# A list scheduler's priorities: one turn a task in place of due times shared by groups

## The chip, the cores and the metric

One core of one Trainium2 chip. The metric is the device time of one execution in microseconds (us). A kernel's time is the median of its runs; the profile is of one execution.

## The reference

Two layers in a row. First, attention with a narrow window: 8 batches, 8 heads, 576 positions, 64 channels. Heads 0 to 3 see the last 32 positions, heads 4 to 7 every fourth of the last 128. Second, a gated feed-forward layer on the 8 heads put side by side.

```python
scores = scale * np.matmul(q, k.transpose(0, 1, 3, 2))
scores = np.where(masks[None, :, :, :], scores, -1000000000.0)
attn = np.exp(scores - np.max(scores, axis=-1, keepdims=True))
attn = attn / (np.sum(attn, axis=-1, keepdims=True) + 1e-09)
x = np.matmul(attn, v)            # then heads side by side: (8, 576, 512)
h = np.maximum(x @ w_in, 0.0)     # 512 -> 1024
conv_out = conv_w[0] * h[s-1] + conv_w[1] * h[s] + conv_w[2] * h[s+1]   # along the positions
gate = 1.0 / (1.0 + np.exp(-conv_out))
out = (h * gate) @ w_out          # 1024 -> 512
```

## The kernel before

The kernel is written as a list of 2032 tasks, each one instruction or a small run of them, with an engine, a cost in us, the tasks it comes after, the buffers it uses and a due time. A planner in the kernel's own Python puts them in one order, and the instructions are emitted in it; every engine then works through its own part in that order.

**Attention** (`attention`, L225 on). A head group is two heads of one batch, four groups a batch, numbered here 0 to 31. Its tasks: loads of `qk` (L231) and `v` (L233) on SP's queue; S, the scores, 72 small matmuls (L243); mask (L254) and max (L256) on VectorE; then for groups 0 to 7 the exponentials by slots on ScalarE, 9 activations with 9 reads of the accumulator (L263), for the others a subtraction, one exponential (L271) and a sum; reciprocal (L276), product (L277) and transpose (L279) on VectorE; V, the values, 80 or 84 small matmuls (L295). V's result leaves PSUM as a rounded half `x..a` (ScalarE, L318) and the rest `x..b`: for groups 0 to 7 by a correction on TensorE (L322) and a ScalarE copy (L325), else by a VectorE subtraction (L330). S and V share one PSUM slot (`att`): the next S or V waits until the one before has been read out, S by the mask, V by `x..a` and `x..b`.

**Feed-forward** (`expert`). The first layer of a batch has 16 groups (8 blocks `fc` of 128 outputs, two halves of the positions), each of 4 pieces of 3 matmuls of 288 columns (L355), a piece for each head group. A group holds one of two PSUM slots `mm` (some of batch 0 take `nn`) until ScalarE's relu to `h` (L362). The gate of a block: the middle tap on ScalarE (L373), two taps on VectorE (L367), sigmoid on ScalarE (L378), product on VectorE (L380), rounded half on ScalarE (L382) and the rest `lo` on VectorE (L384). The second layer has 4 or 5 groups a batch, each of 8 pieces of 3 matmuls of 512 columns (L400), a piece for each block; a group holds one of two slots `nn` until ScalarE's copy `out` (L410), which is then stored from SP's queue. In batch 0 the groups are cut in halves of 256 columns.

**Weights** come as 64-bit numbers and are rebuilt: for each of 8 blocks (`weights`) one load of 1 MB, one Abs (L464) and one copy (L472) on ScalarE, and seven instructions on VectorE (L465 to L479). The conv weights (`few_weights`) are a small load, one Abs and six short VectorE instructions (L435 to L445).

**The planner** (`Planner`). `start` says when a task could start: after the last one on its engine and what it depends on, and when a buffer slot of its pool comes free. `order` takes, engine by engine, the ready tasks whose start is within `WINDOW` (0.25 us) of the earliest, and of these the one with the lowest due time; of the engines the one whose earliest start comes first. Due times come from the table `DUE`, one number for each group of tasks (a batch's first layer, a batch's gates, a head group's softmax and so on), with fixed steps inside a group:

```python
first = min(x[0] for x in at)
s, t = min((x for x in at if x[0] <= first + self.WINDOW), key=lambda x: (x[1].due, x[0]))
```

Tasks are made in this order: weights of the first layer, conv weights, weights of the second layer, the 32 head groups, the 8 batches of the feed-forward part.

Of the kernel before, what the change touches and what calls it, by code (L numbers as in the profile page):

```python
# [56 lines left out]
QK = 2 * S + 32  # L57
# [3 lines left out]
DUE = {  # L61
    "first": (74.70, 81.70, 357.10, 189.80, 929.80, 83.60, 71.70, 1180.10),
    "gated": (93.60, 342.20, 358.10, 9.30, 1117.90, -60.20, -25.30, 36.00),
    "second": (24.50, 424.40, 452.80, 855.50, 1126.50, 1620.90, 1602.90, 1506.70),
    "weights": (82.70, 1550.20, 2380.40, 91.90, 97.30, -18.10, 171.90, 69.10),
    "fetch": (69.90, 42.80, -64.40, -60.40, 72.60, 97.70, 1233.60, 1550.60),
    "conv": 351.60,
    "scores": ((20.00, 1789.40, 129.10, 41.40), (1611.70, 17.90, -51.70, 73.80), (403.50, 353.80, 96.90, 65.70), (270.80, 69.10, 12.90, 80.10), (837.10, -73.40, 77.90, 140.80), (49.80, 977.60, -11.00, 940.00), (1183.10, 95.90, -34.70, 1535.50), (-103.80, 98.20, 411.50, 1557.60)),
    "softmax": ((6.00, -38.50, 7.80, 431.60), (-12.40, 25.50, 0.40, -12.70), (462.70, 1197.90, 365.00, 75.40), (1485.50, 93.40, -17.30, 1003.90), (41.70, 95.80, 1003.50, 910.00), (-44.30, 1543.80, 79.70, 1832.30), (155.80, 89.90, 461.20, 95.80), (94.80, 301.00, -37.60, 31.70)),
    "values": ((842.50, -107.30, -8.70, 6.60), (-23.40, 4.00, 78.20, 43.70), (-4.50, -87.40, -34.50, 89.10), (3.90, 19.10, 32.20, 128.20), (29.70, 66.00, 347.10, -61.20), (-8.50, 1.60, 347.80, 17.20), (961.30, 71.70, 1044.10, 41.10), (22.90, 1623.60, 1475.90, 138.10)),  # L70
    "queries": ((-194.00, -340.50, -87.70, -64.20), (-95.90, 10.40, 59.30, -61.10), (22.90, 138.40, 114.70, 206.60), (959.30, 835.80, 807.00, 1024.00), (1038.20, 1322.20, 1022.30, 1286.00), (1424.90, 492.20, 1554.20, 1412.20), (1489.70, 1710.00, 973.30, 1772.10), (1810.40, 2547.40, 2385.70, 1573.80)),
    "runs": ((-49.30, -20.50, -64.40, -5.70), (40.70, 36.00, 37.60, -38.70), (33.20, 97.00, 48.60, 47.50), (945.80, 351.90, 61.40, 98.30), (456.80, 1101.70, 167.50, 1221.90), (1380.70, 843.50, 1173.90, 1550.10), (1874.10, 1571.80, 1233.90, 1624.20), (1797.40, 2410.30, 1564.00, 1555.00)),
}
# [9 lines left out]
class Task:  # L83
    def __init__(self, engine, cost, due, run, after, uses, table):
        self.engine, self.cost, self.due, self.run, self.table = engine, cost, due, run, table
        self.after, self.uses, self.end = [t for t in after if t is not None], list(uses), None
        for b in self.uses:
            b.left += 1


class Planner:
# [38 lines left out]
    def order(self):  # L130
# [9 lines left out]
        while len(done) < len(self.tasks):  # L140
            best = None
            for e, ts in ready.items():
# [5 lines left out]
                s, t = min((x for x in at if x[0] <= first + self.WINDOW), key=lambda x: (x[1].due, x[0]))  # L148
# [26 lines left out]
def attn_moe(ctx: ExitStack, tc: tile.TileContext, qk_p, qk_d, v_p, v_d, w_in, w_out, conv, mask, out):  # L175
# [49 lines left out]
    def attention(b, p):  # L225
        due, soft, val = SCORES[b][p], SOFTMAX[b][p], VALUES[b][p]
# [4 lines left out]
        lq = plan.add("SP", QK * 0.0017, QUERIES[b][p], lambda: nc.sync.dma_start(  # L231
            out=qk.t, in_=(qk_p, qk_d)[kind][b, p % 2]), uses=[qk])
        lv = plan.add("SP", 1.35, RUNS[b][p], lambda: nc.sync.dma_start(  # L233
# [14 lines left out]
        last = plan.add("PE", 0.75, due, scores, [lq], [qk, sc, s], "S")  # L248
# [5 lines left out]
        last = plan.add("DVE", 0.75, soft + 0.0, lambda: nc.vector.tensor_tensor(  # L254
            out=flat(), in0=scored(), in1=masked, op=ALU.add), [last], [sc, s])
        last = plan.add("DVE", 0.755, soft + 0.5, lambda: nc.vector.tensor_reduce(  # L256
            out=m.t, in_=flat(), axis=AX.X, op=ALU.max, negate=slotwise), [last], [s, m])
        if slotwise:
            last = plan.add("ACT", 0.23, soft + 1.0, lambda: nc.scalar.mul(out=m.t, in_=m.t, mul=SCALE), [last], [m])
# [6 lines left out]
            last = plan.add("ACT", 3.1, soft + 1.5, exps, [last], [s, m, z], "exp")  # L266
            last = plan.add("ACT", 0.23, soft + 2.1, lambda: nc.scalar.add(out=z.t, in_=z.t, add=1e-9), [last], [z])
        else:
            last = plan.add("DVE", 0.755, soft + 1.0, lambda: nc.vector.tensor_tensor(
                out=flat(), in0=flat(), in1=wide(m.t), op=ALU.subtract), [last], [s, m])  # L270
            last = plan.add("ACT", 0.685, soft + 1.5, lambda: nc.scalar.activation(  # L271
                out=flat(), in_=flat(), func=AF.Exp, scale=SCALE), [last], [s], "exp")

            last = plan.add("DVE", 0.765, soft + 2.0, lambda: nc.vector.tensor_reduce(
# [57 lines left out]
        return [plan.add("DVE", 0.77, val + 1.5, low, [last], [tv, x])]  # L332


    TERMS = ((0, 0), (0, 1), (1, 0))
# [241 lines left out]
```

## Time and profile before

| | |
|---|---|
| median of 3 runs | 520.24 us |
| the three runs | 517.2, 520.24, 523.06 us |
| the profiled execution's own time (its span, first to last instruction) | 517.2 us |
| TensorE matmuls busy | 489.6 us, 7464 matmuls |
| VectorE busy | 389.6 us, 552 instructions |
| ScalarE busy | 302.9 us, 623 instructions |
| bytes moved by DMA | 50.96 MB, 99 GB/s on average |

PE is TensorE, PEld its weight loads, DVE is VectorE, ACT ScalarE, SP the engine whose queue holds the loads and stores (SPq). Matmuls are pipelined and their ends are modelled, so a short wait of TensorE may not show as idle time; the distance from one matmul's start to the next one's does show it.

### The profile page before, as it was taken

To read this page: it belongs to the slowest core of one execution; us is meant where nothing else is said; L and a number is where in the kernel's file an instruction comes from. 1 tells how busy PE (TensorE), PEld (TensorE's weight loads), DVE (VectorE), ACT (ScalarE), POOL (GpSimd) and SP (SyncE) were. 2 spreads that over 40 slices of the span, in tenths; PEclk is the share of its full clock that TensorE was granted. 3 is DMA by queue.
4 is the path that set the end of the run, shared out by engine and by line. 5 is a ranking of instruction groups with operands and counts; after the bars stand their busy time and mean duration, and the time that the engine had idled before them with its cause. 6 is when DMAs were issued, how large, how long until landed. Compare 5 with 4: busy or idle time off the path is not lost.

```text
span 517.2 us, 16516 instructions
## 1 busy us (share of the span) xinstructions
PE 489.6 (95%) x7464; PEld 435.8 (84%) x7464; DVE 389.6 (75%) x552; ACT 302.9 (59%) x623; POOL 1.4 (0%) x27
## 2 busy tenths in 40 slices
PE   3379999999999999999999999999999999999996
PEld 2278999999778998799878997899977899889985
DVE  4998999999986999739970599738999479318800
ACT  5967989738432777158741686438632388327710
POOL 1000000000000000000000000000000000000000
PEclk9999999999999999999999999999999999999999
DMA  8866442212255420412132213421244200110011
GB/s 302 292 210 249 166 158 99 69 41 69 90 161 162 135 80 20 151 53 91 53 105 72 68 50 109 142 82 50 95 126 126 74 1 1 42 42 1 1 61 41
DMA packets 16549, 50.96 MB, mean 99 GB/s; under 512 B 2016, under 2 KB 3168, under 8 KB 15456
## 3 DMA queue, kind: packets, MB, share of 16 engines
q1 hardware_dynamic: 16336, 49.84, 28.9%
q8 instruction: 58, 0.95, 0.8%
q10 hardware_dynamic: 144, 0.08, 0.1%
q14 instruction: 11, 0.09, 0.1%
HBM read 40.48 MB, written 9.44 MB: 97 GB/s over the span
## 4 chain that ended last, share of the span: by engine, by line
PE 88%; ACT 8%; DMA 2%; DVE 1%; issue 1%; ACTq 0%
PE nn L400 38%; PE mm L355 36%; PE att L295 6%; PE att L243 5%; ACT s L263 3%; PE nn L355 3%; ACT c L378 1%; ACT L378 1%; DMA qk<-in_qk_p_dram 1%; PE att L322 1%; DMA v<-in_v_d_dram 1%; ACT h L362 0%; DVE c L380 0%; ACT t L464 0%; DVE c L367 0%
## 5 line engine op out<-in xcount | busy, mean ns | idle before, releaser
L400 PE MATMUL nn<-wo,g 128*128 128x512 f32 (+1 forms) x960 | 210.9, 375 | 0.0
L400 PEld LDWEIGHTS nn<-wo,g 128*128 128x128 f32 x960 | 164.6, 188 | 32.1 <-ACT out L410 0.4
L367 DVE SCALAR_TENSOR_TENSOR c<-h,conv_sb,c 128x576 f32<-128x576 f32 x128 | 103.2, 814 | 42.5 <-ACT c L373 41.5
L362 ACT ACTIVATE h<-mm 128x288 f32<-128x288 f32 x120 | 48.1, 406 | 36.4 <-PE mm L355 36.3
L410 ACT COPY out<-nn 128x512 f32<-128x512 f32 (+1 forms) x40 | 21.7, 542 | 63.0 <-PE nn L400 59.2
L355 PE MATMUL mm<-x6a,wi 128*128 128x288 f32 x192 | 54.5, 298 | 0.2 <-ACT h L362 0.2
L380 DVE TENSOR_TENSOR c<-c,h 128x576 f32<-128x576 f32 x64 | 47.7, 756 | 6.8 <-ACT c L378 6.0
L382 ACT CAST g<-c 128x576 fp32r<-128x576 f32 x64 | 42.6, 672 | 17.3 <-DVE c L380 17.2
L373 ACT ACTIVATE c<-h,conv_sb 128x576 f32<-128x576 f32 x64 | 49.6, 777 | 3.7 <-DVE g L384 2.2
L378 ACT ACTIVATE c<-c 128x576 f32<-128x576 f32 x64 | 43.1, 683 | 12.4 <-DVE c L367 11.6
L384 DVE TENSOR_TENSOR g<-c,g 128x576 fp32r<-128x576 f32 x64 | 47.8, 756 | 2.4 <-ACT g L382 1.4
L295 PEld LDWEIGHTS att<-pt,v 32*64 32x64 f32 x2624 | 32.2, 135 | 18.0 <-issue 7.9
L243 PE MATMUL att<-qk 64*32 64x64 f32 x2304 | 33.3, 238 | 12.4 <-DMA qk<-in_qk_p_dram 7.4
L243 PEld LDWEIGHTS att<-qk 64*32 64x32 f32 x2304 | 27.4, 112 | 19.7 <-DVE s L254 5.4
L295 PE MATMUL att<-pt,v 32*64 32x64 f32 (+1 forms) x2624 | 35.9, 235 | 7.8 <-DVE z L276 5.2
L355 PE MATMUL mm<-x2a,wi 128*128 128x288 f32 x144 | 40.9, 299 | 1.0 <-issue 1.0
L355 PE MATMUL mm<-x3a,wi 128*128 128x288 f32 x144 | 40.8, 299 | 0.2 <-ACT h L362 0.2
L355 PE MATMUL mm<-x1a,wi 128*128 128x288 f32 x144 | 40.3, 296 | 0.0
L355 PEld LDWEIGHTS mm<-x6a,wi 128*128 128x128 f32 x192 | 36.1, 188 | 0.9 <-ACT h L362 0.4
L355 PE MATMUL mm<-x5a,wi 128*128 128x288 f32 x128 | 36.4, 299 | 0.2 <-ACT h L362 0.2
L355 PE MATMUL mm<-x0a,wi 128*128 128x288 f32 x112 | 32.4, 306 | 0.0
L355 PE MATMUL mm<-x6b,wi 128*128 128x288 f32 x96 | 28.4, 296 | 0.0
(119 smaller groups left out, 775.9 us busy)
## 6 DMA issues: line engine op xcount, KB each, us to landing
qk<-in_qk_p_dram SPq DMA_DIRECT2D x16, 592.0 KB, 4.0
qk<-in_qk_d_dram SPq DMA_DIRECT2D x16, 592.0 KB, 4.1
out_dram<-out SPq DMA_DIRECT2D x28, 256.0 KB, 2.0
v<-in_v_d_dram SPq DMA_DIRECT2D x16, 384.0 KB, 3.3
v<-in_v_p_dram SPq DMA_DIRECT2D x16, 384.0 KB, 3.4
raw<-in_w_in_dram SPq DMA_DIRECT2D x4, 1024.0 KB, 6.9
raw<-in_w_out_dram SPq DMA_DIRECT2D x4, 1024.0 KB, 6.0
out_dram<-out SPq DMA_DIRECT2D x16, 128.0 KB, 2.3
```

Of the source, the lines that this page charges most:

```text
L243: nc.tensor.matmul(sc.t[quad * 32:quad * 32 + 32, o:o + W], qk.t[hd * 64:hd * 64 + 64, q0:q0 + 32], qk.t[hd * 64:hd * 64 + 64, S + q0:S + ...
L295: nc.tensor.matmul(tv.t[hd * 64:hd * 64 + 64, o:o + hi - lo], v.t[quad * 32:quad * 32 + 32, i, hd * 64:hd * 64 + 64], pt.t[quad * 32:quad ...
L355: nc.tensor.matmul(ps.t[:, 0:HALF], wi[jw][fc // 2][:, fc % 2, k], x[k].t[jx][:, hf * HALF:hf * HALF + HALF], start=(k == 0 and i == 0), s ...
L362: relu.append(plan.add("ACT", 0.4, due + 1.6 * u + 1.6, lambda fc=fc, hf=hf, ps=ps: nc.scalar.activation(out=h[fc].t[:, 1 + hf * HALF:1 + ...
L367: nc.vector.scalar_tensor_tensor(out=c[fc].t, in0=h[fc].t[:, k:S + k], scalar=conv_sb[:, k, fc:fc + 1], in1=c[fc].t, op0=ALU.mult, op1=ALU ...
L373: t = plan.add("ACT", 0.777, d, lambda fc=fc: nc.scalar.activation(out=c[fc].t, in_=h[fc].t[:, 1:S + 1], func=AF.Copy, scale=conv_sb[:, 1, ...
L378: t = plan.add("ACT", 0.686, d + 1.0, lambda fc=fc: nc.scalar.activation(out=c[fc].t, in_=c[fc].t, func=AF.Sigmoid), [t], [c[fc]], "sigmoid")
L380: t = plan.add("DVE", 0.755, d + 1.5, lambda fc=fc: nc.vector.tensor_tensor(out=c[fc].t, in0=c[fc].t, in1=h[fc].t[:, 1:S + 1], op=ALU.mult ...
L382: hi = plan.add("ACT", 0.675, d + 2.0, lambda fc=fc: nc.scalar.copy(out=half(fc, 0), in_=c[fc].t), [t, *(done[fc] if odd else [])], [c[fc] ...
L384: lo = plan.add("DVE", 0.755, d + 2.5, lambda fc=fc: nc.vector.tensor_tensor(out=half(fc, 1), in0=c[fc].t, in1=half(fc, 0).bitcast(F32), o ...
L400: nc.tensor.matmul(ps.t[:, 0:n], g[k // 2].t[:, k % 2, jg, c0:c0 + 128], w.rearrange("p h c -> p (h c)") if hf is None else w[:, hf], star ...
L410: last = plan.add("ACT", 0.582 if hf is None else 0.37, out_due + 8 * cost * (u + 1), lambda ps=ps, o=o, n=n: nc.scalar.copy(out=o.t[:, 0: ...
```

## The change

`DUE` goes, and with it the due time of every `plan.add`. A table `TURNS_OF` takes its place: 2032 different whole numbers from 0 to 2031, one for each task in the order in which tasks are made. `add` gives the task its turn, and `order` takes the lowest turn where it took the lowest due time. Costs, dependences, buffers and the rules of `start` stay, and so do the instructions of every task. The table's first numbers below are the 40 tasks of the first layer's weights, then 8 of the conv weights (1, 4, 6, 7, 8, 12, 14, 18), 40 of the second layer's weights, then the head groups, 15 numbers each for groups 0 to 7 (group 0: 2, 28, 11, ...; group 1: 0, 38, 3, ...).

```diff
-DUE = {
-    "first": (74.70, 81.70, 357.10, 189.80, 929.80, 83.60, 71.70, 1180.10),
-    "gated": (93.60, 342.20, 358.10, 9.30, 1117.90, -60.20, -25.30, 36.00),
...
-}
+TURNS_OF = (
+    117, 138, 147, 156, 162, 169, 154, 159, 171, 188, 78, 113, 120, 122, 125, 135, 112, 115, 132, 136, 5, 33, 47, 53,
+    54, 60, 20, 22, 59, 68, 50, 83, 87, 92, 97, 104, 73, 84, 105, 107, 1, 4, 6, 7, 8, 12, 14, 18, 152, 178, 208, 219,
+    230, 238, 181, 197, 245, 260, 192, 250, 258, 266, 274, 282, 256, 287, 298, 308, 271, 303, 327, 392, 398, 405, 360,
+    367, 408, 430, 315, 413, 421, 446, 452, 460, 418, 436, 463, 469, 2, 28, 11, 17, 19, 23, 25, 36, 39, 42, 44, 55,
+    58, 61, 67, 0, 38, 3, 9, 10, 13, 15, 24, 26, 29, 30, 70, 82, 85, 86, 16, 72, 27, 32, 34, 37, 40, 49, 62, 63, 71,
+    90, 94, 99, 102, 31, 88, 46, 52, 56, 66, 69, 89, 91, 93, 101, 106, 108, 114, 118, 21, 95, 35, 41, 45, 48, 51, 65,
+    76, 77, 81, 121, 123, 129, 133, 43, 109, 137, 140, 144, 149, 153, 174, 180, 184, 191, 200, 204, 222, 229, 141,
...
+    2029, 2030, 2031,
+)
...
-    def add(self, engine, cost, due, run, after=(), uses=(), table=None):
-        t = Task(engine, cost, due, run, after, uses, table)
+    def add(self, engine, cost, run, after=(), uses=(), table=None):
+        t = Task(engine, cost, TURNS_OF[len(self.tasks)], run, after, uses, table)
...
-                s, t = min((x for x in at if x[0] <= first + self.WINDOW), key=lambda x: (x[1].due, x[0]))
+                s, t = min((x for x in at if x[0] <= first + self.WINDOW), key=lambda x: (x[1].turn, x[0]))
...
-        last = plan.add("PE", 0.75, due, scores, [lq], [qk, sc, s], "S")
+        last = plan.add("PE", 0.75, scores, [lq], [qk, sc, s], "S")
```

All other lines of the diff take a due time out of a `plan.add` in the same way.

## Rows read from the trace of the kernel before

**Rows 1.** The page: span; busy time, share, instructions; granted clock by slices
```profile
span 517.2 us, 16516 instructions
...
PE 489.6 (95%) x7464; PEld 435.8 (84%) x7464; DVE 389.6 (75%) x552; ACT 302.9 (59%) x623; POOL 1.4 (0%) x27
...
PEclk9999999999999999999999999999999999999999
```
**Rows 2.** Windows of 20 us: busy us of each engine, granted clock, DMA
```profile
0.00:20.00 20.00, 6.95 (x360) 5.55 (x360) 12.41 (x20) 14.06 (x68) 1.41 (x27) 1.00 0.77 276
20.00:40.00 20.00, 12.44 (x366) 11.72 (x366) 19.11 (x32) 14.65 (x50) 0.00 (x0) 1.00 0.74 266
...
80.00:100.00 20.00, 20.00 (x217) 19.36 (x216) 19.84 (x29) 16.50 (x31) 0.00 (x0) 1.00 0.12 43
```
**Rows 3.** The chain that ended last, in order of time: start, us, what
```profile
20.00 3.10 ACT s L263 x18
23.47 3.10 ACT s L263 x18
...
28.30 1.18 ACT t L464
29.59 0.53 ACT x0b L325
30.21 1.54 PE att L295 x63
31.75 1.74 PE mm L355 x6
...
35.69 1.00 PE att L295 x59
...
41.03 0.97 issue
...
43.79 0.90 PE att L243 x58
...
93.06 0.94 PE nn L400 x6
...
101.28 16.96 PE nn L400 x144
...
459.43 25.70 PE mm L355 x192
```
**Rows 4.** VectorE's timeline, start to 94 us: start, us, engine, line, operation
```profile
6.74 0.76 DVE L254 TENSOR_TENSOR s<-att,mask_sb 128x576 f32<-128x576 f32 x1 [0.56 <-PE att L243]
7.53 0.76 DVE L256 TENSOR_REDUCE m<-s 128x9 f32<-128x576 f32 x1
...
9.73 0.76 DVE L256 TENSOR_REDUCE m<-s 128x9 f32<-128x576 f32 x1
10.40 0.69 DVE L473 TENSOR_SCALAR raw<-raw 128x1024 int32<-128x1024 int32 x1
...
35.06 0.17 DVE L436 TENSOR_SCALAR few<-few 128x24 f32<-128x24 f32 x1
...
44.80 0.76 DVE L254 TENSOR_TENSOR s<-att,mask_sb 128x576 f32<-128x576 f32 x1 [1.14 <-PE att L243]
...
92.33 0.76 DVE L384 TENSOR_TENSOR g<-c,g 128x576 fp32r<-128x576 f32 x1
```
**Rows 5.** The timeline of ScalarE and of SP's queue at the start
```profile
6.56 0.30 ACT L487 ACTIVATE minus<-pt 128x128 fp32r<-128x128 f32 x1
...
0.74 0.86 SPq L231 DMA_DIRECT2D qk<-in_qk_p_dram  x2
```
**Rows 6.** DMA issues up to 50 us: KB each, median us to landing
```profile
few_raw<-in_conv_dram SPq DMA_DIRECT2D x1, 24.0 KB, 7.3
```
**Rows 7.** Waits of TensorE's weight loads: us in total, times, longest
```profile
PEld mm L355 <- ACT h L362: 1.3, 3, 0.4
...
PEld nn L400 <- ACT out L410: 0.4, 1, 0.4
```

More of the change, by code (lines that the diff above doesn't have):

```diff
@@ L83, with __init__ @@
 class Task:
-    def __init__(self, engine, cost, due, run, after, uses, table):
-        self.engine, self.cost, self.due, self.run, self.table = engine, cost, due, run, table
+    def __init__(self, engine, cost, turn, run, after, uses, table):
+        self.engine, self.cost, self.turn, self.run, self.table = engine, cost, turn, run, table
         self.after, self.uses, self.end = [t for t in after if t is not None], list(uses), None
@@ L316, in spans @@
                     for c in range(2) for o, m, n in ((0, 0, RUN), (RUN, 0, 16), (RUN + 16, 16, RUN - 16))]
[L318 removed]
+        last = plan.add("ACT", 0.68, lambda: nc.scalar.copy(out=made(x.t[0])[0], in_=made(x.t[0])[1]), [last], [tv, x])
         if HELPED >> (b * NP + p) & 1:
@@ L322, in less @@
                     nc.tensor.matmul(tv.t[:, o:o + a.shape[1]], minus, a, start=False, stop=True, skip_group_check=True)
-            last = plan.add("PE", 0.5, val + 1.2, less, [last], [tv, x], "E")
-            return [plan.add("ACT", 0.68, val + 1.5, lambda: nc.scalar.copy(
+            last = plan.add("PE", 0.5, less, [last], [tv, x], "E")
+            return [plan.add("ACT", 0.68, lambda: nc.scalar.copy(
                 out=made(x.t[1])[0], in_=made(x.t[1])[1]), [last], [tv, x])]
@@ L330, in low @@
             nc.vector.tensor_tensor(out=out, in0=whole, in1=made(x.t[0].bitcast(F32))[0], op=ALU.subtract)
-        return [plan.add("DVE", 0.77, val + 1.5, low, [last], [tv, x])]
+        return [plan.add("DVE", 0.77, low, [last], [tv, x])]
     TERMS = ((0, 0), (0, 1), (1, 0))
@@ L409, in expert @@
                     done[k].append(last)
-            last = plan.add("ACT", 0.582 if hf is None else 0.37, out_due + 8 * cost * (u + 1), lambda ps=ps, o=o, n=n: nc.scalar.copy(
+            last = plan.add("ACT", 0.582 if hf is None else 0.37, lambda ps=ps, o=o, n=n: nc.scalar.copy(
                 out=o.t[:, 0:n], in_=ps.t[:, 0:n]), [last], [ps, o])
@@ L419, in store, with few_weights @@
                     nc.sync.dma_start(out=out[b * S:b * S + 64, :], in_=o.t[64:128, :])
-            plan.add("SP", 1.0, out_due + 8 * cost * (u + 1) + 0.7, lambda a=(c0, o, base, n): store(*a), [last], [o])
-    def few_weights(src, due):
+            plan.add("SP", 1.0, lambda a=(c0, o, base, n): store(*a), [last], [o])
+    def few_weights(src):
         u, t = few
@@ L430, in step @@
         def step(run, after, engine="DVE"):
-            return plan.add(engine, 0.2, due, run, [after])
-        last = plan.add("SP", 0.1, due - 2.0, lambda: nc.sync.dma_start(
+            return plan.add(engine, 0.2, run, [after])
+        last = plan.add("SP", 0.1, lambda: nc.sync.dma_start(
             out=few_raw, in_=src.bitcast(I32).rearrange("p (n t) -> p n t", t=2)))
@@ L457, in weights @@
         bits = lambda x: x().bitcast(I32)
-        load = plan.add("SP", 3.0, fetch, lambda: nc.sync.dma_start(
+        load = plan.add("SP", 3.0, lambda: nc.sync.dma_start(
             out=raw.t, in_=src.bitcast(I32)), uses=[raw])
         def step(cost, after, run):
-            return plan.add("DVE", cost, due, run, after, [raw, tb])
-        last = plan.add("ACT", 1.14, due, lambda: nc.scalar.activation(out=t(), in_=hw(), func=AF.Abs), [load], [raw, tb])
+            return plan.add("DVE", cost, run, after, [raw, tb])
+        last = plan.add("ACT", 1.14, lambda: nc.scalar.activation(out=t(), in_=hw(), func=AF.Abs), [load], [raw, tb])
         last = step(0.69, [last], lambda: nc.vector.tensor_scalar(
@@ L471, in weights @@
             out=bits(t), in0=bits(hw), scalar=-0x40000000, in1=bits(t), op0=ALU.bitwise_and, op1=ALU.bitwise_or))
-        high = plan.add("ACT", 1.14, due, lambda: nc.scalar.copy(out=hi, in_=shaped(t(), hi)), [top], [tb])
+        high = plan.add("ACT", 1.14, lambda: nc.scalar.copy(out=hi, in_=shaped(t(), hi)), [top], [tb])
         left = step(0.69, [load], lambda: nc.vector.tensor_scalar(
```

75 lines of the change are left out of this document (29 added, 46 removed), and 90 rows, old and new, of the table TURNS_OF.

## The prediction

> **What bounds the kernel now.** I read the head of the page first. TensorE is busy 489.6 of 517.2 us, VectorE 75%, ScalarE 59%, and the granted clock is full in every slice [rows 1]. The windows of 20 us place the idle rest: TensorE is busy 6.95 us in the first window and 12.44 us in the second, 20 of 20 in the window from 80 to 100 us [rows 2]. So most of the 27.6 us without a matmul lie before about 30 us.
>
> The chain of waits shows what holds it there. ScalarE's exponentials of the first heads (18 instructions, a group each 3.47 us from start to start, 20.00 to 23.47) end in `x0b` at 29.59, and only then does TensorE's second value product begin, at 30.21 [rows 3]; the attention has one PSUM slot, so that product (task V of head group 1) waits for the copies out of group 0's. From there the chain is nearly all TensorE.
>
> VectorE is a second, hidden bound. It is busy 19.84 of 20 us from 80 to 100 us [rows 2]. The second-layer stretch of 93.06 us starts as VectorE's last gate instruction (92.33 + 0.76 = 93.09) ends, and takes 0.94 us for 6 matmuls where undisturbed ones take 16.96/144 x 6 = 0.71 [rows 3, 4]. An earlier TensorE start would thus be worth nothing unless VectorE's order also lets it through.
>
> Nothing but order changes, so the sum needs only this: how much earlier does TensorE start its unbroken work, does VectorE's order follow, and what new waits come in.
>
> **The change part by part.** The table has 2032 different numbers, one a task, in order of creation, and every task has a higher turn than those it needs. I read each engine's order off it. TensorE's total is the same: the same tasks, and 118 changes between score, value and full-array matmuls in both orders.
>
> *ScalarE before the first long stretch.* Of the heads' exponentials, before runs groups 1, 0, 4, 2, 3 and then `x0b`. In the table the turns are 15 (group 1), 25 (0), 40 (2), 51 (4), then 67 for `x0b` and 69 for group 3. So one group of exponentials, 3.47 us, moves behind `x0b`; so does the Abs of the weights' fourth block (turn 83), 29.59 - 28.30 = 1.29 us with a small one of the conv weights behind it [rows 3]. Taken away: 4.76 us.
>
> *The conv weights.* Their load moves from 13th to second on SP's queue, their Abs to the head of ScalarE, and three of their VectorE instructions (turns 6 to 8) ahead of the first mask (turn 9). ScalarE is free at 6.56 + 0.30 = 6.86 [rows 5]. Abs and three VectorE instructions at about 0.21 each (0.17 busy and a gap) [rows 4] put the first mask at about 7.7, not 6.74: 1.0 us late for everything behind it. That holds if the load lands by 6.86. The two first loads of before are issued within 0.74 to 1.60 us [rows 5]; this load took 7.3 us where it stood behind others [rows 6], which would be 8.5 and put the mask 2.6 us late. I take 1.0, because only one load stands ahead of it now and the heads that need that load have their first mask at 6.74 in before.
>
> By the Trainium skill (DMA: Bandwidth & Descriptors, "Queues, rings and completion order") each engine takes the descriptors of a ring in order, so a small load should wait for what stands ahead of it and no longer; the sum by that rule is the same 1.0, against 2.6 by the 7.3 us. No run here shows the load in second place yet.
>
> *TensorE's start.* `x0b` comes at 29.59 - 4.76 + 1.0 = 25.8 and ends near 26.4; value product 1 starts at 26.5 instead of 30.21. The next one needs `x1b`, now behind the displaced exponentials: 26.4 + 3.47 + 0.53 (`x1a`, as long as `x0b`) + 1.18 (Abs) + 0.53 = 32.1, against 35.69 [rows 3]: 3.6 us. From there to the score product at 43.79, before needs 8.10 us, of which 0.97 is a stall in which nothing that the profile shows is waited for [rows 3]. The table has another product (V of group 4) in that place behind the same work (12 first-layer pieces, 5 S, 4 V). With the stall it comes at 40.2, without at 39.2. TensorE gains 3.6 to 4.6 us; I take 3.9, nearer the end that keeps the stall.
>
> *VectorE's order.* Take the piece that closes batch 0's gates, the last gate `lo` (fc = 7), and count what stands ahead of the second-layer matmuls that need it. Before: 110 first-layer pieces, 14 half second-layer pieces, 9 S, 8 V, 8 corrections on TensorE; 124 VectorE instructions. By the table: 121, 13, 9, 8, 8; and 128. A first-layer piece is 25.70/192 x 3 = 0.402 us, a half second-layer one 16.96/144 x 3 = 0.353 [rows 3]. So TensorE has 11 x 0.402 - 0.353 = 4.07 us more to do before it needs that gate. VectorE has four more weight instructions ahead (0.69 us each for three of them by the row of 10.40, and one of 1.22 by the planner's cost), about 3.3 us; but back to back dependent neighbours, which start 0.79 us apart (6.74 to 7.53) where independent ones start 0.67 apart (9.73 to 10.40) [rows 4], fall from 45 to 21 of these: 24 x 0.12 = 2.9 us back. Net 0.4 us more. VectorE itself starts 1.0 us late, of which three conv instructions (0.6) are work done early. And 1.14 us that it idled for a score product at 44.80 [rows 4] need not return. So VectorE allows TensorE to be earlier by 4.07 - 0.4 - 0.4 = 3.3 at the least and by 4.4 with the idle time back. That holds the 3.9 of the start, with little to spare. The 0.23 us by which the stretch at 93.06 is too long [rows 3] goes if TensorE no longer runs into the gates: up to 0.3.
>
> *Finer interleaving.* In the table TensorE goes from one accumulation group to another more often: 433 stretches instead of 326. A group takes a PSUM slot only when ScalarE has emptied it. Counted in TensorE's own work, no first-layer group of before takes its slot less than 1.3 us after the last matmul of the group two earlier; in the table 16 do (10 below 1.0 us). Of second-layer groups 2 did, now 5. So 19 places are new. The two of before cost at most 0.4 us together (0.2 each), the 76 first-layer ones that were below 1.65 us three waits of 1.3 us of weight loading in all, 0.02 each [rows 7]. That is 0.4 to 3.8 us; I take 0.7, as the table still has ScalarE's copy next in its order at those places. Beyond 130 us I find no loop from TensorE through VectorE and back that is tighter than before.
>
> *Table loads.* ScalarE changes between exponential and sigmoid 13 times by the table, 17 before. ScalarE is idle 41% of the time [rows 1], so I cost this at nothing; the cover is TensorE's queue of ready pieces, and without it each would be a wait of some tenths like those in [rows 7].
>
> Sum: 3.9 + 0.3 - 0.7 = 3.5 us off the profiled 517.2, that is 513.7. That execution is the fastest of three, 3.04 under their median of 520.24; I take the same distance: 516.7.
>
> **The rivals.** *PSUM slots decide, slower than before.* Nothing speaks against short leads costing 0.2 each but the low number of waits before. At 0.2 us in 19 places the 4.2 of gain falls to 0.4 (519.8); at above 0.22 it is gone, and at 0.5 (ScalarE inside a 1.2 us conversion when its copy is due) the kernel ends 9.5 - 4.2 = 5.3 us slower, at 525.5.
>
> *The array stays slow for longer.* The six matmuls at 31.75 take 1.74 us where 0.80 is normal [rows 3]: near 0.24 us for 288 columns is 1.2 GHz, though the granted clock reads 1.00 [rows 2]; what went before was an almost idle array. With the new order TensorE waits again before value product 2: 26.5 + 1.54 + four pieces at 0.8 ends at 31.3, the product starts at 32.1, 0.8 us later. If that keeps the slow pace for the four pieces and the product behind it, 4 x 0.4 + 0.5 = 2.1 us are lost: 518.8. A conv load that lands at 8.5 gives nearly the same, 1.6 less gain: 518.3. The Trainium skill (TensorE: Matmul & The Clock Gate, "Part 1: The HAM clock gate") has the array start at half rate and sustained activity release it, which by itself favours this rival; the trace agrees that the first long stretch starts slow, and does not show what a wait of 0.8 us in it does.
>
> *More comes back than counted.* Without the 0.97 stall and with all of VectorE's idle time, the start gives 4.6, and with 0.3 and no new PSUM wait 4.9; waits on loads that fall away can add a few tenths: 5.5, or 514.7.
>
> *The order is not what the table says.* The scheduler takes the lowest turn only among tasks that can start within 0.25 us of the first. If that undid the turns, the time would stay at 520.2. The turns keep every dependence, which speaks against it.
>
> **How the numbers follow.** Forecast 0.54, larger gain 0.17, slow array or late load 0.12, PSUM waits 0.14, old order 0.03. The likeliest gives 516.7. A measurement of this kernel tells about 1%, 5.2 us, from no change; the three times of before spread by 5.9. Faster by over 1% means under 515.0: the larger gain for two thirds and the forecast's low edge for a third, 0.11 + 0.18 = 0.29. Slower by over 1% takes PSUM waits near 0.5 us, 0.07. Within 1%: 0.64. The range runs from 512.0 (the larger gain, and a median 2.7 us nearer the fastest run) to 520.8 (PSUM waits of 0.25).
>
> **What would show it.** Right: value product 1 starts near 26.5 us, the fourth one (head group 4) near 40; the first mask near 7.7; `x0b` before the fourth exponentials end; VectorE still full at 80 to 100 us; TensorE's last matmul about 3.5 us earlier, with the distance won before 45 us and kept. Wrong: a first mask beyond 8.5; more than 2 us of waits of the first layer on ScalarE's `h`; TensorE waiting for gates at 90 to 110 us; the distance of 45 us shrinking after 60 us.

## The result

The changed kernel takes 513.46 us (513.07 to 516.55, four runs) where the kernel before takes 520.31 (four runs): a ratio of 0.9886, 95% interval 0.9853 to 0.9918. In a second comparison it was 513.46 against 520.16, 0.9873 (0.9848 to 0.9899). Forecast were 516.7 us and a sum of 3.5 us; 6.85 us came off.

The profiled execution of the changed kernel is the slowest of its four: a span of 514.7 us, where the others have 511.2 to 511.8. Its page, span and busy time:

```profile
span 514.7 us, 16534 instructions
...
PE 487.6 (95%) x7464; PEld 434.8 (84%) x7464; DVE 383.5 (75%) x552; ACT 295.9 (57%) x619; POOL 1.4 (0%) x27
```

Work and shares are those of [rows 1]; ScalarE has 4 instructions less, its table loads (17 before, 13 now). The windows of 20 us (busy us of PE, PEld, DVE, ACT, POOL, granted clock, DMA share, GB/s):

```profile
0.00:20.00 20.00, 6.59 (x349) 5.51 (x350) 12.88 (x25) 13.99 (x69) 1.41 (x27) 1.00 0.83 289
20.00:40.00 20.00, 15.28 (x437) 13.95 (x427) 17.57 (x26) 15.14 (x51) 0.00 (x0) 1.00 0.69 232
40.00:60.00 20.00, 18.95 (x478) 17.50 (x462) 19.00 (x27) 17.22 (x61) 0.00 (x0) 1.00 0.69 241
...
80.00:100.00 20.00, 18.94 (x147) 18.71 (x146) 19.45 (x28) 15.26 (x28) 0.00 (x0) 1.00 0.17 58
```

Beside [rows 2], the gain is in the second window, 15.28 us of matmuls for 12.44; but 80 to 100 us is no longer full (in a second profile, run `e1_after` below, it is: 20.00). TensorE's timeline shows both (in brackets the idle time before an instruction, and what ended it; L377 is the value product, L436 the first layer, L325 the score product):

```profile
27.21 1.53 PE L377 MATMUL att<-pt,v 32*64 32x32 f32 x84 [0.78 <-issue]
...
32.64 1.06 PE L377 MATMUL att<-pt,v 32*64 32x32 f32 x80 [0.73 <-ACT x1b L407]
...
39.72 1.10 PE L377 MATMUL att<-pt,v 32*64 32x32 f32 x84
...
81.50 0.40 PE L436 MATMUL mm<-x4a,wi 128*128 128x288 f32 x1 [1.06 <-ACT h L443]
...
168.92 0.96 PE L325 MATMUL att<-qk 64*32 64x64 f32 x72 [1.47 <-DMA qk<-in_qk_d_dram]
```

Value product 1 starts at 27.21 for 30.21, product 2 at 32.64 for 35.69, the fourth at 39.72 where the other kernel had a score product at 43.79 [rows 3]. TensorE's waits in total (us, times, longest):

```profile
PE att L325 <- DMA qk<-in_qk_d_dram: 6.9, 4, 2.6
...
PE mm L436 <- ACT h L443: 1.8, 2, 1.1
...
PEld mm L436 <- ACT h L443: 2.5, 3, 1.3
```

**One measure for all runs.** Below, the *lag* of TensorE at a point is the start of the task there, less the planner's costs of all TensorE work ahead of it (its costs for a change between kinds of matmul included). All kernels have the same work, so lags at equal work can be compared: a wait raises the lag by its length, and a difference in lag at the end is one of time. (A lag can also fall, where the planner's costs are a little high, in all kernels alike.) (Values from each run's profiled execution. The kernel before stands twice, the second time as run `e2_before`; so does the changed one, as `e1_after`.)

| kernel | after 21 us of work | 52 | 146 | 475 | time, median |
|---|---|---|---|---|---|
| before | 27.6 | 28.0 | 29.6 | 30.2 | 520.3 |
| before, again | 26.5 | 26.9 | 28.3 | 30.2 | 520.9 |
| changed | 23.5 | 25.7 | 28.7 | 27.8 | 513.5 |
| changed, again | 23.5 | 25.9 | 27.1 | 25.5 | 513.5 |
| `e3_start` | 21.9 | 24.0 | 25.8 | 26.3 | 516.0 |
| `e4_rest` | 27.4 | 27.5 | 30.1 | 28.5 | 517.3 |
| `e5_loads` | 21.9 | 23.8 | 24.0 | 22.4 | 511.5 |
| `e7_vector` | 27.7 | 30.7 | 37.7 | 36.7 | 525.5 |
| `e9_undo_scalar` | 25.9 | 28.1 | 30.1 | 28.6 | 517.7 |
| `e10_only_scalar` | 30.6 | 30.9 | 32.4 | 34.0 | 524.3 |
| `e11_relu_first` | 25.8 | 26.0 | 29.0 | 29.4 | 519.6 |

The reader sees three things in the first four rows. The start brings 3.0 to 4.1 us (26.5 and 27.6 to 23.5); kernels below with the same start order (`e3_start`, `e5_loads`) came to 21.9, so a profile's start varies by some 1.6 us from run to run. Of this gain only 0.9 to 1.2 are left after 146 us of work. And from there to the end the kernel before loses 0.6 to 1.9, while the changed one wins 0.9 to 1.6. The forecast had the first of these only.

At the end the two pairs of profiles differ by 2.4 and 4.7 us, less than the medians: the profiled executions of the changed kernel took 516.55 and 514.25 us, more than its median, that of `e2_before` 518.95, less than the median of the kernel before. So below, what a part of the order is worth is taken from the times, and where it arises is read from the traces.

### The profile page after: what moved, and what is told of

It reads as the page before. It is cut to its first block, busy times and chain, and to the rows that moved or that the text cites. A ratio compares the mean times of both kernels' runs of the same rounds, so it can differ in the third digit from the quotient of the medians.

```text
span 514.7 us, 16534 instructions
## 1 busy us (share of the span) xinstructions
PE 487.6 (95%) x7464; PEld 434.8 (84%) x7464; DVE 383.5 (75%) x552; ACT 295.9 (57%) x619; POOL 1.4 (0%) x27
## 3 DMA queue, kind: packets, MB, share of 16 engines
q1 hardware_dynamic: 16336, 49.84, 29.4%
## 4 chain that ended last, share of the span: by engine, by line
PE 83%; DMA 8%; DVE 5%; ACT 1%; issue 1%; SPq 0%; ACTq 0%; DVEq 0%
PE nn L480 40%; PE mm L436 34%; PE att L325 5%; PE att L377 5%; DMA qk<-in_qk_d_dram 4%; DMA raw<-in_w_out_dram 2%; DMA raw<-in_w_in_dram 1%; DMA qk<-in_qk_p_dram 1%; DVE pt L361 1%; DVE s L359 1%; DVE c L448 1%; DVE t L547 0%; DVE t L550 0%; ACT t L544 0%; DVE raw L555 0%
## 5 line engine op out<-in xcount | busy, mean ns | idle before, releaser
L480 PE MATMUL nn<-wo,g 128*128 128x512 f32 (+1 forms) x960 | 213.8, 373 | 0.0
L448 DVE SCALAR_TENSOR_TENSOR c<-h,conv_sb,c 128x576 f32<-128x576 f32 x128 | 101.9, 812 | 20.6 <-ACT c L453 19.9
L464 DVE TENSOR_TENSOR g<-c,g 128x576 fp32r<-128x576 f32 x64 | 47.6, 754 | 26.9 <-ACT g L462 26.2
L436 PE MATMUL mm<-x4a,wi 128*128 128x288 f32 x192 | 54.2, 300 | 1.2 <-ACT h L443 1.1
L325 PEld LDWEIGHTS att<-qk 64*32 64x32 f32 x2304 | 27.6, 112 | 26.3 <-issue 7.6
L325 PE MATMUL att<-qk 64*32 64x64 f32 x2304 | 33.5, 238 | 17.2 <-DMA qk<-in_qk_d_dram 6.9
L436 PE MATMUL mm<-x2a,wi 128*128 128x288 f32 x176 | 49.7, 299 | 0.0
L436 PE MATMUL mm<-x0a,wi 128*128 128x288 f32 x144 | 40.9, 301 | 0.7 <-ACT h L443 0.7
L377 PEld LDWEIGHTS att<-pt,v 32*64 32x64 f32 x2624 | 32.1, 135 | 11.1 <-issue 6.6
L436 PE MATMUL mm<-x1a,wi 128*128 128x288 f32 x144 | 40.2, 296 | 0.0
L361 DVE STREAM_TRANSPOSE pt<-s 128x576 f32<-128x576 f32 x32 | 24.8, 775 | 18.5 <-PE att L377 17.7
L377 PE MATMUL att<-pt,v 32*64 32x64 f32 (+1 forms) x2624 | 35.7, 236 | 2.7 <-issue 1.1
L436 PEld LDWEIGHTS mm<-x4a,wi 128*128 128x128 f32 x192 | 35.9, 188 | 2.6 <-ACT h L443 1.5
L436 PE MATMUL mm<-x6a,wi 128*128 128x288 f32 x128 | 36.2, 298 | 0.0
L436 PEld LDWEIGHTS mm<-x2a,wi 128*128 128x128 f32 x176 | 33.0, 188 | 0.7
```

The costliest lines, as they stand in the source:

```text
L325: nc.tensor.matmul(sc.t[quad * 32:quad * 32 + 32, o:o + W], qk.t[hd * 64:hd * 64 + 64, q0:q0 + 32], qk.t[hd * 64:hd * 64 + 64, S + q0:S + ...
L361: last = plan.add("DVE", 0.775, lambda: nc.vector.transpose(out=pt.t.rearrange("p (a k) -> p a k", k=W), in_=flat()), [last], [s, pt])
L377: nc.tensor.matmul(tv.t[hd * 64:hd * 64 + 64, o:o + hi - lo], v.t[quad * 32:quad * 32 + 32, i, hd * 64:hd * 64 + 64], pt.t[quad * 32:quad ...
L436: nc.tensor.matmul(ps.t[:, 0:HALF], wi[jw][fc // 2][:, fc % 2, k], x[k].t[jx][:, hf * HALF:hf * HALF + HALF], start=(k == 0 and i == 0), s ...
L448: nc.vector.scalar_tensor_tensor(out=c[fc].t, in0=h[fc].t[:, k:S + k], scalar=conv_sb[:, k, fc:fc + 1], in1=c[fc].t, op0=ALU.mult, op1=ALU ...
L464: lo = plan.add("DVE", 0.755, lambda fc=fc: nc.vector.tensor_tensor(out=half(fc, 1), in0=c[fc].t, in1=half(fc, 0).bitcast(F32), op=ALU.sub ...
```

## Experiments

### The two kernels again, and each half of the order

`e1_after` and `e2_before` are the two kernels unchanged. In `e3_start` only the kernel before's first 700 tasks stand in the relative order of the new table, in `e4_rest` only what follows the new table's first 400 turns:

```diff
 # e3_start
-order of the first 700 tasks: by due time
+order of the first 700 tasks: as in TURNS_OF
 # e4_rest
-TURNS_OF, its first 400 turns
+the same 400 tasks in the order of the kernel before
```

> The changed kernel again, beside the kernel before on the same chip, with a second profile. My theory (the gain is made before 45 us and kept): ratio 0.990 to 0.994, TensorE's distance to its own work about 4 us less than before at 45 us and still 3 to 4 us less at the end. Rival (the order also removes small waits all along): ratio 0.985 to 0.989, and the distance grows by less than 1 us from 45 us to the end where the kernel before grows by 2.5 to 3. If the first profile was typical (1.2 us at 81 us, 1.5 us at 169 us lost to waits), both waits come back here.

> The kernel before, unchanged, as the control and for a second profile: ratio 0.997 to 1.003 by every theory. If the pace of the second layer's matmuls (0.2334 us before, 0.2290 in the changed kernel's first profile) is a matter of the chip, it is the same here as in the run of the changed kernel; if it belongs to the order, it is 0.233 here.

> The first 700 tasks of the order before stand in the new table's order, the other 1332 as before. My theory (start decides): ratio 0.990 to 0.993, the same as the changed kernel. Rival (waits all along): about two thirds of the changed kernel's gain, ratio 0.990 to 0.992 with the changed kernel at 0.986, the distance of TensorE to its own work growing by 2 us or more after 100 us as before.

> The reverse: the first 400 tasks of the new order stand in the order before, the others by the new table. My theory: no gain, ratio 0.998 to 1.002. Rival: a third to a half of the changed kernel's gain, ratio 0.993 to 0.996, with TensorE's distance growing by less than 1 us after 100 us.

Measured beside the kernel before at 520.16 us: 513.46 (0.9873); 520.94 (1.0015, 0.9995 to 1.0035); 516.00 (0.9923, 0.9902 to 0.9944); 517.34 (0.9945, 0.9923 to 0.9966). The start is worth 520.16 - 516.00 = 4.2 us, the rest 2.8; together 7.0 of 6.7. So the size of the start was right, and the rival holds for the rest: behind the start the order brings time too, which the sum did not have.

### ScalarE's part undone

First with the scheduler free to rearrange the rest (`e6_scalar`), then with every engine's order written out, so that nothing else moves (`e9_undo_scalar`, `e10_only_scalar` and `e11_relu_first` are made in this way; without an edit it gives each kernel's own order and buffers).

```diff
 # e6_scalar, e9_undo_scalar: ScalarE's order in the changed kernel
 exp 4
-x0a, w hi, add 4, m 3, x0b, exp 3, x1a, w abs, x1b, add 3
+add 4, m 3, exp 3, add 3, x0a, w hi, w abs, x0b, x1a, x1b
```

> The changed kernel with ScalarE's order of before in its first 31 tasks: the fourth group's exponentials run ahead of x0a, the weights' Abs ahead of x0b. TensorE, VectorE and the queue keep their turns. Theory (the prediction's term: 4.76 us of ScalarE work stood ahead of x0b): value product 1 starts 4.0 to 4.8 us later than the 27.0 of the changed kernel, near 31.4; the distance stays to the end, time near 513.5 + 4.2 = 517.7, ratio 0.995. Rival (VectorE's order or the order of loads makes the start, ScalarE's part is hidden): value product 1 within 1 us of 27.0, ratio 0.987 to 0.989. In between, the part of the 4.76 us that shows is the term's true size.

> The changed kernel with the order of every engine written out as it is, so that the scheduler rearranges nothing, and one part undone: on ScalarE group 3's exponentials stand ahead of x0a again and the weights' Abs ahead of x0b, as in the kernel before. In the earlier run of this kind the scheduler rearranged the other engines too. Theory (the prediction's term of 4.76 us sets the start): value product 1 starts 4 to 5 us later than the 25.2 to 27.2 of the changed kernel, the distance at the score product of group 6 is 4 us and the time 513.5 + 4 = 517.5, ratio 0.9935 (0.992 to 0.996). Rival (the loads' waits near 49, 56 and 167 us take in part of the delay, since a later TensorE no longer runs into them): 4 us later at product 1, but only some 2 us at the end, time 515.5, ratio 0.990. Second rival (VectorE's later gates turn it into more): the time over 520, as in the earlier run.

`e6_scalar` took 527.87 us (1.0146, 1.0112 to 1.0181). It changes part of the computation, which part was not found, so nothing below rests on it. `e9_undo_scalar`, in which nothing but ScalarE's order differs, took 517.74 us (0.9963, 0.9943 to 0.9984): 4.3 us more than the changed kernel by the medians, as the theory had it. TensorE's timeline (L341 is the value product, L368 the correction):

```profile
27.14 1.12 PE L368 MATMUL att<-x0a,minus 128*128 128x160 f32 x4 [5.10 <-ACT x0a L364]
29.81 1.54 PE L341 MATMUL att<-pt,v 32*64 32x32 f32 x84 [1.56 <-issue]
...
35.17 1.07 PE L341 MATMUL att<-pt,v 32*64 32x32 f32 x80 [0.73 <-ACT x1b L371]
...
42.11 1.10 PE L341 MATMUL att<-pt,v 32*64 32x32 f32 x84
```

The correction waits 5.10 us for `x0a`; in the changed kernel's two profiles that wait is 0.7 and 1.1. The prediction's 4.76 us are the right term, and within the changed kernel they are worth 4.3 in the median. The profiles show less of it: product 2 starts 2.5 us later than the 32.64, the fourth one 2.4, and the lag at group 6's scores is 2.4 to 2.9 more, where the expectation had 4.

### ScalarE's part alone

```diff
 # e10_only_scalar: ScalarE's order in the kernel before
-m 3, exp 3, add 3, x0a, w hi, w abs, conv abs, x0b, x1a
+x0a, w hi, x0b, m 3, exp 3, add 3, x1a, w abs, conv abs
```

> The kernel before with the order of every engine written out as it is, and the prediction's ScalarE part done alone: group 3's exponentials behind x0b, the Abs of the weights' fourth block and of the conv weights behind x1a. VectorE, TensorE and the queue keep the order of before. Theory of the prediction (ScalarE's order makes the start, VectorE has no part in it before the gates): value product 1 near 26.5 instead of 30.2, product 2 near 32, 3.5 us gained at the score product of group 5. Rival (VectorE works strictly in order and has group 3's reciprocal ahead of group 2's transpose: it waits for the displaced exponentials and holds product 2 back): product 1 2 to 3.5 us earlier, but VectorE idle some 3 us near 30, product 2 2 us later than the 35.6 of before, and the kernel 2 to 5 us slower than before: ratio 1.004 to 1.010.

524.26 us, 1.0092 (1.0056 to 1.0127): 4.1 us slower than before, as the rival had it. VectorE's timeline (L322 reciprocal, L325 transpose):

```profile
26.60 0.77 DVE L325 STREAM_TRANSPOSE pt<-s 128x576 f32<-128x576 f32 x1
31.27 0.22 DVE L322 RECIPROCAL z<-z 128x9 f32<-128x9 f32 x1 [3.90 <-ACT z L313]
...
36.65 0.77 DVE L325 STREAM_TRANSPOSE pt<-s 128x576 f32<-128x576 f32 x1
```

VectorE stands idle 3.90 us at group 3's reciprocal, which waits for the displaced exponentials. Behind it in VectorE's order are a block of weights and group 2's transpose (36.65). Value product 2 starts at 38.41, 2.7 us later than the 35.69 of [rows 3]. It needs that transpose, done at 37.42, and `x1b`, which comes last (ScalarE's timeline, then TensorE's; L516 is the copy of the weights, L371 the copy `x1b`):

```profile
36.77 1.05 ACT L516 CAST wi<-t 128x1024 fp32r<-128x1024 f32 x1 [3.81 <-DVE t L514]
37.72 0.63 ACT L371 CAST x1b<-att 128x576 fp32r<-128x576 f32 x1
```
```profile
38.41 1.47 PE L341 MATMUL att<-pt,v 32*64 32x32 f32 x80 [5.08 <-ACT x1b L371]
```

`x1b` stands behind the copy of the weights, and that copy waits for the same late VectorE. The edit left the copy ahead of `x1b`, as in the kernel before; the new table has it behind `x2b`. So about 0.9 us of the delay (38.35 less 37.42, an estimate) belong to this place and not to VectorE's transpose.

Product 1 starts at 28.49, not 26.5: product 0 still starts at 23.72, after its `v` load (issued 17.35, 6.23 us), which in the changed kernel is issued at 9.40, and product 1 waits 1.40 us for its own, issued at 25.27 (13.33 in the changed kernel).

TensorE stands idle from 33.33 to 38.41, and the granted clock falls to 0.50 (1.2 GHz) from 35.1 to 42.0. The slower steps cost some 1.5 us in this profile (an estimate: product 2 takes 1.47 us for 1.07, the six matmuls behind it 1.74 for 0.80). The loss does not hang on that: two of the six executions have a mean granted clock of 1.000 and took 525.71 and 526.94 us.

### VectorE's part undone

```diff
 # e7_vector: VectorE's order in the changed kernel, first 45 tasks (core)
-recip 2, ..., transpose 2, w, recip 4, ..., transpose 4
+recip 4, ..., recip 2, ..., transpose 4, w, w, transpose 2
```

> The changed kernel with VectorE's order of before in its first 45 tasks or so (the reciprocal, product and transpose of head group 4 ahead of group 2's and 3's, one conv instruction later); ScalarE, TensorE and the queue keep their turns. Theory (the prediction gave VectorE no part in the start): value product 1 within 0.5 us of 27.0, the fourth one within 1 us of 39.7, ratio 0.987 to 0.989. Rival (each engine's order is needed, since group 3's probabilities come late from VectorE): product 1 as before within 0.5 us, the later products up to 3.6 us late, first-layer work held behind them; ratio 0.994, time near 517.

525.46 us, 1.0090 (1.0062 to 1.0118). The rival was right on the mechanism and far too small. Product 1 is early (25.69), and then TensorE waits at every later head (its timeline, L391 the correction, L364 the value product, L423 the first layer):

```profile
38.70 0.66 PE L391 MATMUL att<-x3a,minus 128*128 128x160 f32 x4 [0.73 <-ACT x3a L387]
40.09 1.09 PE L364 MATMUL att<-pt,v 32*64 32x32 f32 x80 [0.73 <-ACT x3b L394]
41.90 1.54 PE L391 MATMUL att<-x4a,minus 128*128 128x144 f32 x6 [0.73 <-ACT x4a L387]
44.18 0.61 PE L423 MATMUL mm<-x4b,wi 128*128 128x288 f32 x1 [0.38 <-ACT x4b L394]
```

The table above has it: lag 27.7 after 21 us of work, the whole start gone, and 37.7 after 146. But the run does not isolate VectorE. The scheduler, free here to rearrange the rest, put value product 4 (36.87) ahead of 3 (40.09) on TensorE, with no first-layer piece between them, and group 4's copies ahead of group 3's on ScalarE. And behind these waits the granted clock fell to 0.50 (1.2 GHz) from 41.0 to 47.8 us. The windows, columns as above:

```profile
40.00:45.00 5.00, 3.80 (x90) 3.35 (x91) 4.86 (x6) 3.23 (x5) 0.00 (x0) 0.60 0.83 251
45.00:50.00 5.00, 5.00 (x96) 4.55 (x95) 4.17 (x6) 2.31 (x7) 0.00 (x0) 0.72 0.86 303
```

That is some 2 us (an estimate: the correction at 41.90 takes 1.54 us for 0.84, the scores at 45.68 1.33 for 0.97, nine first-layer matmuls 0.24 for 0.13 each). The mean granted clocks of all four executions are 0.989 to 0.993, against 0.999 to 1.000 in the changed kernel. How much of the whole is VectorE's alone stays open.

### The conv weights late

```diff
 # e8_conv
-conv load: second; its Abs first on ScalarE; three of its VectorE instructions ahead of the first mask
+conv load: 11th; its Abs behind x0a; its VectorE instructions behind the weights' fourth block
```

> The changed kernel with the conv weights late again: their load 11th on the queue, their Abs behind x0a, their VectorE instructions behind the weights' fourth block of before's place. Theory of the prediction (their early place costs 1.0 us): first mask 0.8 to 1.0 us earlier than the 6.85 of the changed kernel or at the 6.74 of before, value product 1 0.8 to 1.0 earlier, near 26.1, time 0.8 us less, ratio 0.9855. Rival (the Abs slips in while ScalarE and VectorE wait for the first scores, cost 0.1): first mask 6.74, value product 1 within 0.4 of 27.0, time within 0.5 us of 513.5; if the late place only moves the same work behind x0a, where it is on the path, up to 0.7 us slower, ratio 0.988.

513.46 us, 0.9859 (0.9831 to 0.9887): no change that can be told from none. The early place costs 0.1 us, by the changed kernel's own timelines (ScalarE's Abs, then VectorE):

```profile
6.08 0.22 ACT L515 ACTIVATE few<-few_raw 128x24 f32<-128x24 f32 x1
```
```profile
6.33 0.18 DVE L516 TENSOR_SCALAR few<-few 128x24 f32<-128x24 f32 x1 [0.16 <-ACT few L515]
6.54 0.18 DVE L517 TENSOR_SCALAR few<-few 128x24 int32<-128x24 int32 x1
6.75 0.18 DVE L519 SCALAR_TENSOR_TENSOR few<-few_raw,few 128x24 int32<-128x24 int32 x1
6.85 0.75 DVE L336 TENSOR_TENSOR s<-att,mask_sb 128x576 f32<-128x576 f32 x1
```

The load was issued at 1.18 and had landed at 5.66; the Abs ran at 6.08, ahead of the `minus` copy (6.55), and the three VectorE instructions were done as the first scores came. The first mask starts at 6.85 for 6.74 [rows 4].

### Where the start's gain goes: loads that hold a slot

`qk` has two slots. In `e1_after` the new table lets group 8's load go at 19.38 us though its scores are computed at 113.9; until then groups 6, 7 and 10 share the other slot, and each load is issued only when the score product before it has ended. Its chain:

```profile
43.06 0.91 PE att L325 x58
43.98 0.02 issue
43.99 4.45 DMA qk<-in_qk_d_dram
48.44 0.14 issue
48.58 0.97 PE att L325 x54
49.55 0.02 issue
49.57 6.02 DMA qk<-in_qk_d_dram
55.59 0.14 issue
55.73 0.96 PE att L325 x54
```

Group 26's load (140.02 for 208.5) does the same to group 18, at 168.92 in the timeline above. There the load also stands behind stores on SyncE's queue: the score product before it ends at 162.3, the load is issued at 164.74.

```diff
 # e5_loads: turns of the loads, in the order in which the scores are computed (core)
-group 6: 141, 7: 165, 10: 217, 8: 64, ... 26: 617, ... 31: 1095
+group 6: 64, 7: 141, 10: 165, 8: 217, ... 26: 774, ... 31: 1386
```

> The changed kernel with one thing altered: the loads of the 32 score inputs take their turns in the order in which the score products use them. In the changed kernel the loads of head groups 8 and 26 (and 31) are issued 68 to 94 us before their use and hold one of the two slots all that time, so that groups 6, 7, 14, 15, 18, 13 and 12 share the other slot and their loads start only after the score product before. Theory (the slot that is held makes TensorE wait): the waits ahead of the score products near 49, 56 and 167 us (0.5, 1.7 and 1.1 us in the run above) go, 2 to 3 us in all; time 513.5 - 2.5 = 511.0, ratio to the kernel before 0.982, and group 7's load is issued some 9 us ahead of its use instead of 6. Rival (the loads are late since the queue itself is slow or other loads run beside them): the waits stay within 0.5 us, ratio 0.987. Second rival (these waits are covered, since VectorE's order holds TensorE later anyway): the waits go, and the time stays within 0.7 us of 513.5.

511.46 us (511.18 to 512.51, five runs), 0.9831 (0.9804 to 0.9858): 2.0 us less than the changed kernel's 513.46, and the fastest of all. `e8_conv`, measured in the same comparison with the changed kernel's order of loads, has 513.46 too (512.25 to 513.82). The waits of `e5_loads` and SyncE's queue:

```profile
PE att L312 <- DMA qk<-in_qk_d_dram: 2.6, 1, 2.6
```
```profile
20.44 0.33 SPq L300 DMA_DIRECT2D qk<-in_qk_d_dram  x1
...
42.42 0.33 SPq L300 DMA_DIRECT2D qk<-in_qk_d_dram  x1
```

Of four waits for such loads one is left, at the very start. Group 7's load is issued 10.1 us ahead of its use (52.49), not 6.2, and the lag rises by 2.1 us from 21 to 146 us of work instead of 3.6 to 5.2 (2.6 in `e8_conv`'s profile). Theory and size hold. The kernel before, which issues group 7's load at 16.2 us and group 8's at 43.7 to 44.7, has a rise of 1.8 to 2.0; but it too holds a slot for group 8, until 148, and issues group 6's load only 6.5 us ahead of its use.

### What the rest of the order brings

In the kernel before, at 233, 352 and 419 us, TensorE waits for a relu that stands on ScalarE behind a sigmoid's table load. Its ScalarE timeline at the first of them, and the matmul that waits:

```profile
230.58 1.28 ACT L378 ACT_TABLE_LOAD   x1
231.87 1.26 ACT L378 ACTIVATE c<-c 128x576 f32<-128x576 f32 x2
233.04 0.39 ACT L362 ACTIVATE h<-mm 128x288 f32<-128x288 f32 x1
```
```profile
233.48 0.41 PE L355 MATMUL mm<-x3a,wi 128*128 128x288 f32 x1 [0.19 <-ACT h L362]
```

The first-layer piece before it started at 232.73 and takes 0.40: 0.35 us are lost, of which the profile shows 0.19 as idle. The next piece starts 0.52 us later, so the lag steps up by 0.45 in all.

```diff
 # e11_relu_first: ScalarE's order in the kernel before, batches 3, 5 and 6
-sigmoid 0, sigmoid 1, relu (fc 2, second half)
+sigmoid 0, relu (fc 2, second half), sigmoid 1
```

> The kernel before with the order of every engine written out as it is, and in three places (batches 3, 5 and 6) one relu of the first layer moved on ScalarE from behind the second sigmoid to ahead of it. There the chain of waits shows a sigmoid's table load of 1.28 us ahead of a relu that TensorE waits for, and TensorE's offset steps up by 0.35 us each time (at 233, 352 and 419 us). Theory (these waits are part of what the new order removes behind 145 us): the three steps go, 1.05 us in all, and TensorE's offset at the end is 29.2 instead of 30.2; ratio 0.998 (a measurement hardly tells that, the offsets do). Rival (the step comes from the PSUM slot and the gates behind: the sigmoid that is now 0.4 us later delays its gate): the steps stay or move to the second layer; ratio 1.000.

519.64 us, 0.9996 (0.9971 to 1.0021): by time nothing can be told. By the trace the theory holds: the relu starts at 232.11 between the two sigmoids, and the step in lag at the three places falls from 0.45 us each to 0.00. In the changed kernel these steps are 0.00 too. What hid these 1.4 us in the median stays open; in this profiled execution waits of 0.9 to 1.05 us stand at three other places, two of which cost 0.4 to 0.6 in the kernel before.

A second part is again a held slot. The kernel before loads group 31 at 320 us for a use at 421, so group 30's load waits for the other slot. Its chain in `e2_before`:

```profile
380.01 5.33 DMA qk<-in_qk_d_dram
385.34 0.14 issue
385.48 0.96 PE att L243 x55
```

TensorE idles 1.29 us there, and 1.25 in `e10_only_scalar`, which has the same order; where the load took 3.93 us (the first profile of the kernel before) it idles 0.0. The changed kernel issues that load 7.2 us ahead of its use and doesn't wait.

Third, the last 120 matmuls of 512 columns start 0.2333 us apart before and 0.2291 apart in the changed kernel and in `e4_rest`: 119 x 0.0042 = 0.5 us. This is not an effect of TensorE's order, since `e3_start` and `e11_relu_first`, which have the old order there, run at 0.2291 too. So 1.4, 0.5 and 0 to 1.3 make 1.9 to 3.2 where `e4_rest` measured 2.8. That is a sum of waits read from traces; the one part that was tried alone, the relus, could not be told by time.

## Why the prediction was right and wrong

The measured 513.46 us lies inside the range (512.0 to 520.8), 3.2 us below the likeliest value and among the times faster by over 1%, which had a chance of 0.29.

**The start (took 3.9 us): right, in part by luck.** 3.0 to 4.1 in lag, 4.2 by `e3_start`, 4.3 by the time of `e9_undo_scalar` (2.4 by its lag). Product 1 came at 27.21 (26.5 forecast; 25.2 in the second profile), product 2 at 32.64 (32.1), the fourth at 39.72 (39.2 to 40.2). These places contain 1.0 us for the conv weights that did not come; pauses of TensorE with nothing awaited (0.78 us ahead of product 1, and 1.03 within it in the second profile) filled about the same time. The two errors nearly cancel.

**Why it is so: half wrong.** The working had ScalarE's order as the cause and VectorE's only as a bound at the gates. ScalarE's part is needed but brings nothing alone (`e10_only_scalar`, 4.1 us slower); the table also puts group 2's transpose ahead of group 3's reciprocal on VectorE, the copy of the weights behind `x2b` on ScalarE, and product 0's `v` load at 9.40 us. The sum came out since the table has them all.

**The conv weights (1.0 us): wrong by a factor of ten.** 0.1 us. The step that failed is "ScalarE is free at 6.86": the Abs ran before the last set-up copies, not behind them. The load's place was read rightly: 4.5 us from issue to landing with one load ahead, against the 7.3 of [rows 6]. It landed at 5.66, 0.4 us behind the one load ahead of it (0.74 + 4.56 = 5.30). That agrees with the rule cited from the Trainium skill (DMA: Bandwidth & Descriptors, "Queues, rings and completion order"), that an engine takes the descriptors of a ring in order.

**VectorE's order lets the start through: right.** No wait of TensorE for a gate is in the changed kernel's list, and VectorE is busy 19.45 us from 80 to 100 us (19.91 in the second profile).

**The distance won before 45 us is kept: wrong.** It shrinks from 3.0 to 4.1 us to 0.9 to 1.2 after 146 us of work, which the prediction had named as a sign against it. Held load slots take 2.0 us of it (`e5_loads`). The prediction looked at PSUM slots and VectorE as things that could take the gain back, and never at SyncE's queue beyond the first loads, where the table has group 8's load 94 us ahead of its use.

**Finer interleaving (0.7 us): within its bounds.** The waits for `h` are 1.8 us in the first profile, against 0.6 before; the second profile has none in its list. The largest, 1.06 us at 81.50, lies in the first profile only. The rival with PSUM slots (525.5) is out. *More comes back than counted* (514.7) is nearest by number but not by its reasons: the fourth product came midway between the places with and without the stall, and waits on loads did not fall away but came in.

**Table loads at nothing, and "beyond 130 us no tighter loop": the term that was mis-sized.** The search was for waits that the new order might add, and counted none of those that the old order has and the new one drops: 0.45 us at three places and group 30's load (the pace of the last stretch, 0.5 us, no reading of the order could have given). Behind the start the sum had +0.3 and -0.7, a loss of 0.4, where `e4_rest` measured a gain of 2.8: 3.2 of the 3.35 us between the forecast 3.5 and the 6.85 that came off.

**From span to median (+3.04): wrong reasoning.** The time of a profiled execution lies 1.7 to 2.0 us above its span (516.55 and 514.7; 518.95 and 517.2), so a span of 517.2 is an execution of about 519, not the fastest of the three at 517.2. The sum itself, 513.7 for the span, lies between the 514.7 and 512.4 of the two profiles.

**The slow array for longer: out.** About four pieces of the first layer run at 0.24 us a matmul in both kernels, the pace of 1.2 GHz. The granted clock of 1.00 that the views give there is no measurement: the traces' clock records begin, at full clock, at 30.91 us in the changed kernel (35.45 before), and just there the pace changes (the matmuls at 30.52 and 30.76 are 0.24 apart, those at 31.10 and 31.23 0.13). Product 2 at 32.64 and what follows take their usual time. So one wait of 0.73 us did not bring the half pace back. The granted clock did fall to 0.50 behind several such waits in a row in `e7_vector`, and in a wait of 5.08 us in `e10_only_scalar`. The rule of the Trainium skill (TensorE: Matmul & The Clock Gate, "Part 1: The HAM clock gate"), a slow start that sustained work ends, agrees with the first four pieces; what was drawn from it for a short wait after them did not show.

## What to carry to other kernels

On engines that work strictly in order, a piece of one engine's order is worth only what the others' orders let through: moving ScalarE's exponentials gains 4.3 us with the other orders moved to match, and costs 4.1 without. In a list of priorities, give loads into a pool of few slots the order of their use; one that goes early holds its slot, and every load behind it then starts only when the one before has been consumed. And when a new order is costed, list the waits that the old one has along the whole kernel too, not only those that the new one may add.

## What the runs showed of the hardware that was not expected

- Identical matmuls have two paces: the last 120 of 512 columns start 0.2333 us apart in the kernel before, its repetition and `e10_only_scalar`, and 0.2291 in all other runs, at a granted clock of 1.00. `e11_relu_first` has the same TensorE order as before, so that order isn't the cause; what is stays open.
- A value product can start and stop, or start late, with nothing awaited that the profile shows: 0.78 and 1.03 us at product 1 in `e1_after`, 1.56 in `e9_undo_scalar`, 2.85 in `e8_conv`, 0.45 and 0.63 at 389 us in the kernel before, 1.03 there in `e11_relu_first`. Product 2 came at 31.2 us in `e3_start` and `e5_loads`, and at 32.6 to 33.1 in the two profiles of the changed kernel and in `e8_conv`, at nearly the same start order. It was not explained.
- Loads of the same `qk` shape took 3.3 to 9.1 us to land, with a median of 4.0 to 4.5 in each run. On what this depends was not tried.
- The granted clock fell back to 0.50 in the middle of a kernel: from 35.1 to 42.0 us in `e10_only_scalar`, where TensorE had stood idle since 33.33, and from 41.0 to 47.8 in `e7_vector`, behind its waits ahead of 38.70 and 40.09. In the changed kernel's two profiles it did not.
